# Sixteen tiny copies of zeros behind GpSimd's end-stage stores in a forward and backward decoder step

## The chip, the cores and the metric

The kernel runs on one core of a Trainium2 chip. The core has five instruction streams that run side by side and meet only at semaphores: TensorE (PE), VectorE (DVE), ScalarE (ACT), GpSimd (POOL) and SyncE (SP). Transfers between the chip's memory and the on-chip buffers, and from memory to memory, are carried by sixteen transfer engines. GpSimd and SyncE issue nearly all transfers here. The metric is the device time of one execution in microseconds, and less is better.

## The reference

The reference is one decoder step with adaptive layer norm and the gradient of it. Cut to what matters:

```python
mod = silu(c) @ w_mod                      # six vectors of 1024
sa, ca, ga, sb, cb, gb = split(mod, 6)
h = layernorm(x) * (1 + ca) + sa
q = h @ wq                                 # 32 heads of 128, one query
k, v = k_cache[:, :, -4096:], v_cache[:, :, -4096:]   # of 65536 rows, 4 groups
x = x + ga * (softmax(q k^T / sqrt(128)) v @ wo)
h = layernorm(x) * (1 + cb) + sb
x = x + gb * ((sigmoid(h @ w_gate) * (h @ w_up)) @ w_down)
return x, vjp(x)(grad_out)                 # gradients of ten inputs
```

The gradients of the two caches are as large as the caches, 4 x 65536 x 128 bfloat16 each. Only the last 4096 rows of each group have gradients that are not zero; all other rows must be written with zeros. The weight gradients are outer products of a column and a row.

## The kernel before, in words

**What is written.** Some 186 MB are written and 88 MB read. Most of what is written are the zeros of the two cache gradients, `out_2` (for k) and `out_3` (for v); then come the outer products `out_4` (`wq`), `out_5` (`wo`), `out_6` and `out_7` (`w_gate`, `w_up`), `out_8` (`w_down`) and `out_10` (`w_mod`). The step is for a single token, so all matrix products have one vector on one side.

**Zeros.** `zero` (L184 to 211) writes the zero rows a MiB at a time. The first ten pieces come from an on-chip buffer of zeros; from then on they are copied from memory to memory, out of `zero_src`, a piece of `out_2` that has been filled by then. Six pieces are *narrow*: the cursor that says on which transfer engine the next transfer of few rows starts is reset (L191), a copy of five rows (L193) and one of 60 rows (L197) follow. The pieces are spread over the whole kernel by tables of counts, each tied to a matrix product or a vector instruction that has to be done first. All are written before the end stage.

**The end stage.** From about 512 us on, what is left are weight gradients and the gradients of the live cache rows. Each is made in an on-chip buffer and stored whole, 1 MiB or half of one. These names matter below (line numbers of the profile):

- `sec(j)` (L1249, store at L1253): VectorE makes four of the six sections of row block j of the `w_mod` gradient; GpSimd stores 1 MiB.
- `dwq_tile(j)` (L1299, store at L1301): row block j of the `wq` gradient, 1 MiB.
- `s2(j)` (L1303, store at L1305): the other two sections of the `w_mod` gradient, 512 KiB.
- `grad_kv` (L1282): 32 small matrix products, each copied out of its bank by ScalarE (for v) or by ScalarE and VectorE in turn (for k) at L1292 or L251. A function `between` is called ahead of each one, and it puts other stores between them.
- `kv_store` (L1296, store at L1297): 1 MiB of the finished cache gradient of one group.

For v, `dv_between` runs `sec(4)` and `dwq_tile(0)` ahead of product 8, `sec(5)` and `dwq_tile(1)` ahead of 16, `sec(6)` and `dwq_tile(2)` ahead of 24; four `kv_store` follow, then `sec(7)` and `dwq_tile(3)`. For k, `dk_between` runs:

```python
        if t_ == 4:
            dwq_tile(4)
            s2(0)
            s2(1)
        elif t_ == 10:
            dwq_tile(5)
            s2(2, tail)
            s2(3, tail)
        elif t_ in (18, 25):
            g = (t_ - 4) // 7
            dwq_tile(4 + g, tail)
            s2(2 * g, tail)
            s2(2 * g + 1, tail)
```

`tail` is SyncE's queue; without it a store is GpSimd's. At the end, two `kv_store` of `out_2` are GpSimd's and two SyncE's.

**What sets the order.** Every engine runs its instructions in the order in which they are written down. Buffers are places in one large on-chip area, used again by hand: VectorE waits ahead of an outer product until the store that last read the place has landed. `sec(7)` and then `s2(3)` and `s2(4)` share such a place. The completion semaphores of GpSimd's DMAs form a ring of eight: each DMA takes the next one and first waits until the DMA that had it before has landed, so at most eight of GpSimd's DMAs are under way. SyncE has a ring of eight of its own.

Of the kernel before, what the change touches and what calls it, by code (L numbers as in the profile page):

```python
# [61 lines left out]
def kernel(  # L62
# [26 lines left out]
    nc = tc.nc  # L89
# [19 lines left out]
    def vt(shape, name, dt=FP32):  # L109
        n = shape[1] if dt == FP32 else (shape[1] + 1) // 2  # L110
        if dt not in (FP32, BF16) or n > 48:
            return pool.tile(shape, dt, name=name)
        a = slab[1]
        slab[1] += n
        assert slab[1] <= slab[0].shape[1], slab
        v = slab[0][:, a:a + n]
        return v if dt == FP32 else v.bitcast(BF16)[:, 0:shape[1]]
# [4 lines left out]
    ZW = 4096  # L122
# [15 lines left out]
    def fill_rows(og, g):  # L138
        return og[0, g, 0:SKW, :].rearrange("r d -> (r d)")

    first_rows = fill_rows(out_2, 0).rearrange("(p x) -> p x", p=P)
# [9 lines left out]
    zero_src = flat.pop(0)  # L151
# [6 lines left out]
    narrow = zregions[0:len(NARROW)]  # L158
    zleft = []
# [9 lines left out]
    assert nlen * 2 <= 20  # L169

    keep = [0]
    from_dram = [False]
    zero_rows = zero_src[:, 0:P * ZW // 4].rearrange("i (p x) -> (i p) x", p=P).bitcast(FP8)

# [9 lines left out]
    def zero(n, after=None, big=False):  # L184
        for _ in range(n):
            if len(zleft) <= keep[0]:
                return
            region, narrow_ = zleft.pop(0)
            first = None
            if narrow_:  # L190
                nc.gpsimd.inc_swdge_sem([], [], mode="reset_dge_cursor")  # L191
                n = nlen - ncount.pop()
                first = nc.gpsimd.dma_start(  # L193
                    out=rest[0:NS, 0:nlen * 128].rearrange("p (t x) -> p t x", t=2)[:, :, n * 64:(n + 1) * 64],
                    in_=(zero_rows[0:NS, 0:128].rearrange("p (t x) -> p t x", t=2) if from_dram[0] else
                         zeros[0:NS, 0:64].rearrange("p (t x) -> p t x", t=1).broadcast_to([NS, 2, 64])))
                ins = nc.gpsimd.dma_start(  # L197
                    out=pairs(region[8:P, :].bitcast(FP32)),
                    in_=(pairs(zero_rows[0:120, :]) if from_dram[0] else
                         zeros[0:60, :].rearrange("p (t x) -> p t x", t=1).broadcast_to([60, 2, ZW // 2])))  # L200
            elif big and region.shape[0] == 1:
                ins = nc.gpsimd.dma_start(  # L202
                    out=as_rows(region, BIGP).bitcast(FP32),
                    in_=zero_src[:, 0:P * ZW // 4].rearrange("i (p x) -> (i p) x", p=BIGP).bitcast(FP8))
            else:
                if region.shape[0] == 1:
                    region = as_rows(region, P)
                if from_dram[0]:
                    ins = nc.gpsimd.dma_start(out=pairs(region.bitcast(FP32)), in_=pairs(zero_rows))  # L209
                else:  # L210
                    ins = nc.gpsimd.dma_start(out=region.bitcast(FP32), in_=zeros[:, :])
            if after is not None:
                dep(first or ins, after)
# [26 lines left out]
    def mulv(out, a, b):  # L240
        return tt(out, a, b, ALU.mult)
# [12 lines left out]
    def ttr(out, w, b, acc):  # L254
        return nc.vector.tensor_tensor_reduce(out=out, in0=w, in1=b, scale=1.0, scalar=0.0,  # L255
                                              op0=ALU.mult, op1=ALU.add, accum_out=acc)
# [13 lines left out]
    def matvec_T(blk, cols, name):  # L270
        ncol = cols.shape[2]
        ps = new_acc("mv_" + name)
        for jb in range(KD):
            for nb in range(KD):
                nc.tensor.matmul(ps[:, jb * ncol:(jb + 1) * ncol], lhsT=blk(jb, nb),
                                 rhs=cols[:, nb, :], start=(nb == 0), stop=(nb == KD - 1))
        half = ncol // 2
        v = ps[:, 0:KD * ncol].rearrange("p (j n) -> p j n", j=KD)
        res = vt([P, KD * half], name)
        r = res.rearrange("p (j n) -> p j n", j=KD)  # L280
        cp(r, v[:, :, half:ncol])
        addv(r, r, v[:, :, 0:half])
        return r
# [4 lines left out]
    def outer_dve(out, col, b):  # L288
        return ts(out, b, col, ALU.mult)
# [219 lines left out]
    jobs = []  # L509
# [212 lines left out]
    for g in range(G):  # L722
# [29 lines left out]
        for k in range(2):  # L752
            nc.tensor.matmul(nbank[k][:, :], lhsT=nkb_rows[:, :], rhs=bd[:, 4 * k:4 * k + 4, :].rearrange("p h d -> p (h d)"),
                             start=False, stop=True)
            c0 = (HG * g + 4 * k) * P
# [9 lines left out]
    bq = []  # L765
# [483 lines left out]
    def sec(j):  # L1249
        w5 = g_t[j]  # L1250
        ttr(w5, w5, dmod_b4[:, 3 * D:4 * D], dcs[:, j:j + 1])
        outer_dve(sec_t[j], cs_col[:, j:j + 1], dmod_b4)
        nc.gpsimd.dma_start(out=dwm_view[:, j, 2 * D:6 * D], in_=sec_t[j])  # L1253
# [25 lines left out]
    def kv_out(og, g):  # L1279
        return og[0, g, SKW:, :].rearrange("(p t) d -> p (t d)", t=KT)  # L1280

    def grad_kv(rows, bd, scale, home, engs, between=lambda t_: None):  # L1282
        for t_ in range(KT):
            between(t_)
            tc_, t8 = divmod(t_, 8)
            r = slice(32 * tc_, 32 * tc_ + 32)
            ps = new_ps("ps_kv")
            nc.tensor.matmul(ps[:, :], lhsT=rows[r, t8 * P:(t8 + 1) * P], rhs=bd[r, :], start=True, stop=True,  # L1288
                             tile_position=(32 * tc_, 0))
            o, v = home[:, :, t_ * P:(t_ + 1) * P], ps.rearrange("p (g d) -> p g d", g=G)  # L1290
            if engs[t_ % len(engs)] == "A":
                nc.scalar.activation(out=o, in_=v, func=ACT.Copy, scale=float(scale))  # L1292
            else:
                ts(o, v, float(scale), ALU.mult)

    def kv_store(og, home, g, queue=nc.gpsimd):  # L1296
        queue.dma_start(out=kv_out(og, g), in_=home[:, g, :])  # L1297

    def dwq_tile(j, queue=nc.gpsimd):  # L1299
        outer_dve(dwq_t[j], h1[:, j:j + 1], dq_b)  # L1300
        queue.dma_start(out=dwq_view[:, j, :], in_=dwq_t[j])  # L1301
# [7 lines left out]
    for b in range(2):  # L1309
        do4 = new_ps("do4")  # L1310
        for i in range(KD):
            for a in range(4):
# [4 lines left out]
                       in_=do4.rearrange("q (a h r) -> q a h r", a=4, h=4))  # L1317
# [94 lines left out]
    def dv_between(t_):  # L1412
        if t_ == 8:
            sec(4)
            dwq_tile(0)
        elif t_ == 16:
            sec(5)
            dwq_tile(1)
        elif t_ == 24:
            sec(6)  # L1420
            dwq_tile(2)

    grad_kv(P_b2, DO_bd, 1.0, dv_home, "A", dv_between)
    for g in range(3):
        kv_store(out_3, dv_home, g)
    dln1 = vt([P, KD], "dln1")
    mulv(dln1, dh1, ca1)
    dx0b, _ = layernorm_bwd_col(dln1, ln1, rstd1, "ln1b")
# [2 lines left out]
    bcast(dmod_bf[:, 0:16], 16, dmod_b2, "A")  # L1431
    dcs01 = matvec_T(lambda jb, nb: w01_T[:, nb, jb * P:(jb + 1) * P], dh1_hl, "dcs01")
    kv_store(out_3, dv_home, 3)
    sec(7)
    dwq_tile(3)
    x2 = vt([P, KD], "x2")
    mulv(x2, gb, ffn)
    addv(x2, x2, x1)
# [36 lines left out]
        kv_store(out_2, dk_home, g, nc.gpsimd if g < 2 else tail)  # L1475
    keep[0] = 0
    zero(len(zleft))
    assert not zleft and not narrow and not jobs and not bq

# [1 line left out]
_INS = ['A_x', 'A_k_cache', 'A_v_cache', 'A_wq', 'A_wo', 'B_x', 'B_w_gate', 'B_w_up', 'B_w_down', 'c', 'w_mod', 'grad_out']  # L1481
# [26 lines left out]
```

## Time and profile before

The time is 592.95 us, the median of two runs (592.76 and 593.14).

| What | Value |
|---|---|
| Profiled execution: its time | 593.15 us |
| Profiled execution: its span | 591.4 us |
| PE, DVE, ACT, POOL busy | 426.5, 353.6, 247.9, 147.3 us |
| Bytes moved by DMA, mean rate | 246.05 MB, 416 GB/s |
| Read from and written to memory | 88.52 MB, 185.60 MB |
| GpSimd's queue (q0): packets, MB, share of 16 engines | 26864, 225.98, 94.8% |
| SyncE's and ScalarE's queues (q1, q10) | 4944 and 48 packets, 19.41 and 0.01 MB, 9.3% and 0.0% |

The span reaches from the first instruction to the last; the time also holds what lies around it. A queue's share is the time that its packets took, out of sixteen engines over the whole span; both queues use the same sixteen engines. The time of a store "to landing" runs from its issue to its completion, and so holds the time that it stands in line behind older stores. In the prediction below, a timeline line has start, duration, engine, line in the kernel, operation, tiles, count, and in brackets how long the engine stood idle before it and what ended that. A line of the stretches has the stretch, its length, busy time and instructions of PE, of its weight loads, of DVE, ACT and POOL, then the granted TensorE clock, the share of the DMA engines and GB/s.

### The profile page before, as it was taken

The numbers are of one execution on the slowest core, as the hardware profiler recorded it, in microseconds if no ns is written. First come the engines' busy times: TensorE is split into PE (matmuls) and PEld (weight loads), VectorE is DVE, ScalarE is ACT, GpSimd is POOL, SyncE is SP. The second block draws the span as 40 slices with busy tenths as digits, with TensorE's granted clock in tenths as the row PEclk, the third lists the DMA queues.
The fourth block names the chain that finished last, engine by engine and source line by source line (L and its number), as shares of the span: only waits on it lengthen the run. The fifth ranks groups of instructions, "written<-read, shape, count | busy, mean of one in ns | idle before, by whom it ended". The sixth has DMA issues, their size and how long they took to land.

```text
span 591.4 us, 10184 instructions
## 1 busy us (share of the span) xinstructions
PE 426.5 (72%) x4167; PEld 245.7 (42%) x4196; DVE 353.6 (60%) x644; ACT 247.9 (42%) x398; POOL 147.3 (25%) x250
## 2 busy tenths in 40 slices
PE   3997779999999999997976856767664447075410
PEld 2784433332334545543544645555552435013100
DVE  3665679988830102039371866877986968555750
ACT  2579511554540103411223655666581456084310
POOL 3112214122122212222222321333212533222100
PEclk9998689999999999998997667786876558555555
DMA  8999999999999999999999999999999999999997
GB/s 348 421 418 423 418 457 423 426 432 434 422 401 462 408 444 427 405 433 442 421 377 414 417 412 410 399 409 402 422 418 423 426 426 423 424 419 415 414 416 313
DMA packets 31903, 246.05 MB, mean 416 GB/s; under 512 B 4765, under 2 KB 4765, under 8 KB 16544
## 3 DMA queue, kind: packets, MB, share of 16 engines
q0 software_dynamic: 26864, 225.98, 94.8%
q1 hardware_dynamic: 4944, 19.41, 9.3%
q8 instruction: 33, 0.54, 0.4%
q14 instruction: 14, 0.11, 0.0%
q10 hardware_dynamic: 48, 0.01, 0.0%
HBM read 88.52 MB, written 185.60 MB: 464 GB/s over the span
## 4 chain that ended last, share of the span: by engine, by line
DMA 36%; PE 27%; DVE 18%; ACT 9%; issue 5%; POOL 1%; ACTq 0%; POOLq 0%; DVEq 0%
DMA out_dram<-out_dram 13%; DMA out_dram<-arena 10%; PE n_ps L733 9%; DMA arena<-in_w_mod_dram 6%; DMA arena<-in_B_w_gate_dram 6%; DVE arena L255 5%; PE b_ps L792 4%; DVE arena L251 4%; PE t_ps L687 4%; DVE scr L255 3%; ACT arena L1292 3%; ACT arena L526 2%; DVE arena L238 2%; ACT arena L695 1%; PE tp_k L505 1%
## 5 line engine op out<-in xcount | busy, mean ns | idle before, releaser
L792 PE MATMUL b_ps<-arena 128*128 128x512 bf16 x493 | 115.3, 382 | 2.6 <-ACT arena L936 1.1
L238 DVE TENSOR_TENSOR arena<-arena 128x2048 bf16<-128x2048 bf16 (+1 forms) x67 | 78.2, 1177 | 9.0 <-PE n_ps L733 5.2
L936 ACT COPY arena<-tp_side 128x1024 bf16<-128x1024 bf16 x62 | 60.8, 1017 | 49.7 <-PE tp_side L935 49.0
L792 PEld LDWEIGHTS <-arena 128*128 128x128 bf16 x512 | 48.7, 99 | 57.6 <-issue 4.6
L733 PE MATMUL n_ps<-arena 128*128 128x512 bf16 x247 | 66.5, 389 | 3.4 <-DVE arena L238 2.5
L202 POOL DMA_DIRECT2D out_dram<-out_dram x72 | 35.7, 496 | 129.5 <-PE n_ps L733 49.6
L251 DVE TENSOR_SCALAR arena<-arena,slab 128x3584 bf16<-128x3584 bf16 (+2 forms) x40 | 43.4, 1120 | 24.1 <-DMA out_dram<-arena 24.1
L935 PE MATMUL tp_side<-ident_bf,arena 128*128 128x128 bf16 x496 | 49.7, 265 | 8.9 <-DVE arena L238 4.5
L935 PEld LDWEIGHTS <-arena 128*128 128x128 bf16 x496 | 41.3, 122 | 17.7 <-issue 9.2
L1288 PE MATMUL ps_kv<-arena 32*128 32x512 bf16 x64 | 26.6, 581 | 28.5 <-DVE arena L259 11.7
L695 ACT CAST arena<-t_ps 128x512 bf16<-128x512 f32 x56 | 28.9, 598 | 39.9 <-PE t_ps L687 39.9
L1292 ACT ACTIVATE arena<-ps_kv 128x512 bf16<-128x512 f32 x48 | 25.0, 723 | 38.8 <-PE ps_kv L1288 19.7
L255 DVE CUSTOM_DVE_ANT_0 arena<-arena,scr 128x1024 bf16<-128x1024 bf16 x35 | 40.8, 1219 | 0.2
L733 PEld LDWEIGHTS <-arena 128*128 128x128 bf16 x256 | 21.5, 99 | 35.4 <-issue 18.9
L255 DVE CUSTOM_DVE_ANT_0 scr<-arena,b1k 128x1024 bf16<-128x1024 bf16 x28 | 34.2, 1222 | 3.1 <-DMA arena<-in_B_w_down_dram 2.6
L247 DVE CAST arena<-b_ps 128x512 bf16<-128x512 f32 x6 | 4.1, 692 | 48.9 <-PE b_ps L792 48.9
L209 POOL DMA_DIRECT2D out_dram<-out_dram x32 | 19.5, 610 | 33.6 <-DVE rows_all L238 25.2
L687 PE MATMUL t_ps<-arena 128*32 128x512 bf16 x256 | 24.1, 399 | 3.3 <-ACT arena L756 2.8
L1288 PEld LDWEIGHTS <-arena 32*128 32x128 bf16 x64 | 6.8, 112 | 47.1 <-issue 46.4
L526 ACT COPY arena<-tp_wq 128x1024 bf16<-128x1024 bf16 x23 | 21.4, 1070 | 7.3 <-PE tp_wq L524 7.3
L1073 ACT COPY arena<-tp_ug 128x1024 bf16<-128x1024 bf16 x21 | 20.5, 1007 | 7.5 <-PE tp_ug L1072 7.5
L1049 PE MATMUL fg<-arena,slab 128*32 128x256 bf16 x224 | 15.1, 404 | 8.2 <-DMA arena<-in_B_w_gate_dram 8.2
(266 smaller groups left out, 649.3 us busy)
## 6 DMA issues: line engine op xcount, KB each, us to landing
out_dram<-arena POOLq DMA_DIRECT2D x35, 1024.0 KB, 14.6
out_dram<-out_dram POOLq DMA_DIRECT2D x32, 1024.0 KB, 12.8
out_dram<-arena POOLq DMA_DIRECT2D x16, 896.0 KB, 17.5
out_dram<-zeros POOLq DMA_DIRECT2D x10, 1024.0 KB, 10.3
arena<-in_A_wq_dram POOLq DMA_DIRECT2D x8, 1024.0 KB, 20.9
arena<-in_A_wo_dram POOLq DMA_DIRECT2D x8, 1024.0 KB, 13.7
arena<-in_w_mod_dram POOLq DMA_DIRECT2D x7, 1024.0 KB, 18.9
arena<-in_B_w_up_dram POOLq DMA_DIRECT2D x14, 512.0 KB, 10.1
```

The source lines that it names most:

```text
L202: ins = nc.gpsimd.dma_start(out=as_rows(region, BIGP).bitcast(FP32), in_=zero_src[:, 0:P * ZW // 4].rearrange("i (p x) -> (i p) x", p=BIGP ...
L238: return nc.vector.tensor_tensor(out=out, in0=a, in1=b, op=op)
L251: return nc.vector.tensor_scalar(out=out, in0=a, scalar1=s1, scalar2=None, op0=op0)
L255: return nc.vector.tensor_tensor_reduce(out=out, in0=w, in1=b, scale=1.0, scalar=0.0, op0=ALU.mult, op1=ALU.add, accum_out=acc)
L687: nc.tensor.matmul(ps[32 * hh:32 * hh + 32, :].rearrange("p (j m) -> p j m", j=4), lhsT=N_sb[:, h * P + a:(h + 1) * P - 3 + a:4], rhs=a4[: ...
L695: nc.scalar.copy(out=o, in_=v)
L733: mm = nc.tensor.matmul(nbank[k][:, :], lhsT=k_nat[:, g, t_ * DH:(t_ + 1) * DH], rhs=vp[:, t_ % 2, 4 * k:4 * k + 4, :].rearrange("p h d -> ...
L792: mm = nc.tensor.matmul(bbank[p][k][:, :], lhsT=a4[:, p, h, :], rhs=wo_t[u][:, a, k * 512:(k + 1) * 512], start=(i == 0 and a == 0), stop= ...
L935: nc.tensor.transpose(tp[:, i * P:(i + 1) * P], blk[:, i * P:(i + 1) * P], ident_bf[:, :])
L936: nc.scalar.copy(out=blk if dst is None else dst, in_=tp[:, :])
L1288: nc.tensor.matmul(ps[:, :], lhsT=rows[r, t8 * P:(t8 + 1) * P], rhs=bd[r, :], start=True, stop=True, tile_position=(32 * tc_, 0))
L1292: nc.scalar.activation(out=o, in_=v, func=ACT.Copy, scale=float(scale))
```

## The change

A helper `mark` is added. It issues one copy from memory to memory, on GpSimd's queue: out of `zero_src` into rows 0 to 16 of the first group's zero area in `out_2`, which hold zeros already. Each of the 17 rows has two runs of n elements of two bytes. n is 3 for the first copy and grows by one to 18 for the sixteenth, and each copy has a place of its own. With the first call the engine cursor is reset. A copy with 17 rows is meant to go whole to one transfer engine, and the next copy to the next engine.

The calls stand behind `sec(4)` to `sec(7)`, behind `dwq_tile(0)` to `dwq_tile(3)` and behind the four `kv_store` of `out_3`: twelve in all. Four more follow the last of these, so that there are five in a row ahead of `dwq_tile(4)`. No instruction is taken out. On the other engines the order of instructions is the same; on GpSimd there are seventeen instructions more. Sixteen copies are twice the ring of eight, so the DMAs behind the last copy have the semaphores that they had before. The waits of VectorE and SyncE are for the same stores as before.

```diff
     keep = [0]
+    marks = []
+
+    def mark():
+        if not marks:
+            nc.gpsimd.inc_swdge_sem([], [], mode="reset_dge_cursor")
+        n = 3 + len(marks)
+        c0 = 7 * ZW + 1024 * len(marks)
+        marks.append(n)
+        nc.gpsimd.dma_start(out=first_rows[0:17, c0:c0 + 1024].rearrange("p (k x) -> p k x", k=2)[:, :, 0:n],
+                            in_=zero_src[:, 0:17 * 256].rearrange("i (p k x) -> (i p) k x", k=2, x=128)[:, :, 0:n])
...
     def dv_between(t_):
         if t_ == 8:
             sec(4)
+            mark()
             dwq_tile(0)
+            mark()
         elif t_ == 16:
             sec(5)
+            mark()
             dwq_tile(1)
+            mark()
         elif t_ == 24:
             sec(6)
+            mark()
             dwq_tile(2)
+            mark()
 
     grad_kv(P_b2, DO_bd, 1.0, dv_home, "A", dv_between)
     for g in range(3):
         kv_store(out_3, dv_home, g)
+        mark()
...
     kv_store(out_3, dv_home, 3)
+    mark()
     sec(7)
+    mark()
     dwq_tile(3)
+    mark()
+    mark()
+    mark()
+    mark()
+    mark()
```

## The prediction

> **What bounds the kernel now.** I read the DMA rows of the page first, because the work is mostly stores. Of 16 transfer engines 94.8% of the span goes to the packets of GpSimd's queue and 9.3% to those of SyncE's.
>
> ```profile
> DMA  8999999999999999999999999999999999999997
> q0 software_dynamic: 26864, 225.98, 94.8%
> q1 hardware_dynamic: 4944, 19.41, 9.3%
> q10 hardware_dynamic: 48, 0.01, 0.0%
> ```
>
> The row of tenths stays at nine from the second slice to the last but one, so the sum of bytes over the rate of the engines sets the time, and an instruction that is late costs something only where the engines run dry. Next I cut the end stage into stretches (column after POOL: granted TensorE clock, DMA share, GB/s).
>
> ```profile
> 520.00:530.00 10.00, 9.28 (x19) 1.88 (x19) 5.90 (x6) 9.92 (x21) 2.34 (x3) 0.50 1.02 421
> 555.00:560.00 5.00, 0.37 (x1) 0.10 (x1) 2.37 (x4) 0.00 (x0) 0.00 (x0) 0.50 1.00 413
> 583.00:585.00 2.00, 0.00 (x0) 0.00 (x0) 0.00 (x0) 0.00 (x0) 0.00 (x0) 0.50 1.00 408
> 585.00:587.00 2.00, 0.00 (x0) 0.00 (x0) 0.00 (x0) 0.00 (x0) 0.00 (x0) 0.50 0.87 367
> 587.00:588.00 1.00, 0.00 (x0) 0.00 (x0) 0.00 (x0) 0.00 (x0) 0.00 (x0) 0.50 0.53 221
> 589.00:590.00 1.00, 0.00 (x0) 0.00 (x0) 0.00 (x0) 0.00 (x0) 0.00 (x0) 0.50 0.12 49
> ```
>
> The engines are full to 585 us and then fall out one by one; 0.12 of 16 is two engines that carry the last microsecond. Third comes GpSimd's timeline, with what it waited for.
>
> ```profile
> 525.68 1.02 POOL L1253 DMA_DIRECT2D out_dram<-arena  x1 [7.14 <-DVE arena L251]
> 529.22 1.02 POOL L1253 DMA_DIRECT2D out_dram<-arena  x1 [1.81 <-DVE arena L251]
> 530.41 0.53 POOL L1301 DMA_DIRECT2D out_dram<-arena  x1 [0.18 <-DVE arena L238]
> 536.15 2.10 POOL L1297 DMA_DIRECT2D out_dram<-arena  x4 [5.21 <-ACT arena L1292]
> 540.03 1.02 POOL L1253 DMA_DIRECT2D out_dram<-arena  x1 [1.77 <-DVE arena L251]
> 548.60 0.53 POOL L1301 DMA_DIRECT2D out_dram<-arena  x1 [6.84 <-DVE arena L251]
> ```
>
> Asking for each of these stores alone gives its time from issue to landing: 16.1 us for the first `dwq_tile` (518.0), 11.0 for `sec(5)` (525.7), 12.3 for `dwq_tile(1)` (526.9), 17.6 for `sec(7)` (540.0), 19.7 for `dwq_tile(3)` (541.2). Added to the issues, the landings come every 2.5 to 2.8 us from 528.9 to 557.6, as 1 MiB at 416 GB/s (2.5 us) must. What they wait for is each other. The chain says last where a landing holds an engine:
>
> ```profile
> 540.03 17.57 DMA out_dram<-arena
> 557.60 0.03 issue
> 557.63 6.28 DVE arena L251 x9
> ```
>
> `s2(3)` on VectorE overwrites the buffer of `sec(7)` and may start when that store has landed; the last four stores follow from there at 570.1 to 571.1, and land by 590.5. At 570 the engines still have about 8 us of older work, so that chain could slip by some microseconds for nothing. The bound is the transfer engines.
>
> **The change, part by part.** Nothing is removed. Added on GpSimd: one cursor reset, and sixteen copies of 17 rows by two runs of 3 to 18 bfloat16, thus 34 packets of 6 to 36 bytes each.
>
> *GpSimd's time.* The reset is one instruction; the six like it take 18 ns each. A narrow copy of 10 runs takes 601 ns (row of L193), a plain one of three rows 522 (L417); I take 0.6 us, so sixteen are 9.6 us. Between 516.8 and 571 GpSimd is busy some 15 us, so it has the room. If it had not, each copy would delay the store behind it by 0.6 us.
>
> *Waits.* In the program every GpSimd DMA takes one of eight completion semaphores in turn and first waits for that semaphore's last user. The copies take places in this ring, so from `dwq_tile(0)` on a big store waits for the big store four before it, not eight. With the old landings the new issues are: `sec(6)` when `sec(4)` lands, 531.4 (529.2 before); `dwq_tile(2)` 534.1 (530.4); the four stores of `kv_store` 536.7, 539.2, 542.0, 544.7 (536.2 to 537.7); `sec(7)` 547.3 (540.0); `dwq_tile(3)` 549.8 (541.2); after the last five copies `dwq_tile(4)` at 557.6 (548.6), with `s2(0)`, `s2(1)` and `dwq_tile(5)` behind it in GpSimd's queue up to 561. Nobody but the end waits for these four. Until `sec(7)`, three or four big stores are in flight at each of these issues. Before, at 525.7, there were four as well, and the stretch 520 to 530 above shows a share of 1.02 and 421 GB/s: four are enough. So `sec(7)` lands where it did, and VectorE's chain holds, each later only by what the copies take from the engines.
>
> *The one thin place.* When `dwq_tile(4)` is let go, only `dwq_tile(3)` (2.5 us of work) and SyncE's first half-megabyte store (553.3 to 562.3) are under way. An issue takes 0.5 to 1.0 us on GpSimd and then has to reach the engines, which I bound by as much again; so 1.0 to 2.0 us against a cover of 2.5 and more. I take 0.2 us; without the cover it is 2.0. SyncE's waits are unchanged.
>
> *The engines' time.* If the copies go to the sixteen engines in turn, each engine gets 34 small packets once, and a completion for each of sixteen copies (the page counts 4765 packets under 512 B for about 280 DMAs, some 16 or 17 each). What a tiny store packet costs no row shows. From below: the mean packet of q1 is 19.41 MB / 4944 = 3926 B and takes 9.3% x 16 x 591.4 us / 4944 = 178 ns, of which the bytes need 150 at the 26.1 GB/s of one engine (422 GB/s at a share of 1.01), so 28 are left; in q0 it is 334 ns for 8412 B, 12 left. Bytes aside, 34 x 12 ns = 0.4 us, or nothing if they fit between others. From above: q10's 48 packets, 256 B and less, round to 0.0%, at most 0.05% x 16 x 591.4 = 4.7 us, 99 ns each, so 3.4 us; they are the nearest row. A packet cannot well cost more than q1's 178 ns, 6.1 us, unless each waits for memory. I take the middle of 28 and 99, 63 ns: 34 x 63 = 2.1 us, and 16 completions x 28 ns = 0.4 us. Every engine gets the same, so the two that end last end 2.5 us later.
>
> [...]
>
> *Sum.* 2.5 + 0.2 = 2.7 us on the profiled execution's 593.15 us (span 591.4 and 1.75 around it): 595.85. Its time is 0.2 above the median of the runs, 592.95, so for the median I say 595.65, rounded 595.7.
>
> **Rivals.**
>
> *The copies vanish (not slower).* For it: the share runs to 1.02, so packets of the two queues overlap, and 34 x 21 B is no traffic. Against it: full engines have no idle time to give before 585 us. Price: 0 to 0.4 us, so 592.9 to 593.3. It decides if a tiny packet costs under 12 ns.
>
> *Each tiny write waits.* [...] For it: `out_dram<-out_dram` has memory at both ends, as the copies have, unlike q10. Against it: those 1 MiB copies run at full share, so their reads overlap. At q1's 178 ns it is 6.1 + 0.4 + 0.2 = 6.7 us: 599.7; at double that price, about 606.
> [...]
>
> *Too few in flight (slower).* If the engines need the seven stores of the steady stretch (latency 17.5 us there) and not four, the twelve stores after 518 flow at 4 MiB in 17.5 us, 4.4 us each and not 2.5: 12 x 1.9 = 23 us, so 616. For it: GpSimd's issues really come up to 9 us later. Against it: the 1.02 at 525 us with four in flight. It decides once landings stand more than 2.7 us apart while four are out.
>
> *The copies don't go round (slower).* If the cursor stays, all sixteen meet on one engine: 544 x 63 ns = 34 us there, partly hidden if it is an early one, so about 620 to 627. No row tells for or against it: the kernel's six pairs of a five-row and a 60-row copy go through the same cursor, and the share of 1.0 to 585 us shows only that they left no engine far behind. If a copy were spread over all engines, each would still get 34 packets and the forecast stands.
> [...]
>
> **How the numbers follow.** Forecast 0.57, with a range of its own from 594.0 to 597.5; vanishing 0.17; waiting writes 0.19; too few in flight 0.04; one engine 0.03. The range 592.6 to 600.6 takes in the forecast's whole range, most of the vanishing case and the lower half of the waiting one, some 0.8 together. A measurement of this kernel can tell about 2%, 11.9 us, from no change. Over that lie the last two rivals, nearly whole, and the far end of the waiting one: slower 0.06. Faster by so much needs bytes taken away, and none are: 0.01. Within 2%: 0.93.
>
> **What the profile of the changed kernel would show.** Right: GpSimd's issues of `sec(7)` and `dwq_tile(4)` near 548 to 550 and 558 to 561, each after a wait for a landing; landings of big stores falling to 10 to 11 us after issue; a DMA share of 1.0 through 585 us; q0 about 800 packets more, the last engines done near 592.5. Wrong: a share under 0.97 between 555 and 565 (the thin place is real), landings over 2.7 us apart with four stores out, the end at 591.5 or less (the copies vanish), at 596 or more (they wait).

## The result, and the profile after

The changed kernel takes 601.61 us (median of two runs, 601.31 and 601.90) against 592.95: a ratio of 1.0144, 95% interval 1.0127 to 1.0161, or 8.7 us more where 2.7 were forecast. It lies just above the stated range. The profiled span is 599.5 us, 8.1 more. All times here and below are of undisturbed executions; two of the four of the kernel with double the runs took 992 and 1984 us, and they are left out.

The page, with the same rows as before, and the row of packet counts:

```profile
DMA  9999999999999999999999999999999999999997
DMA packets 32415, 246.10 MB, mean 410 GB/s; under 512 B 5266, under 2 KB 5277, under 8 KB 17056
q0 software_dynamic: 27376, 226.03, 94.6%
q1 hardware_dynamic: 4944, 19.41, 9.4%
```

The engines look as busy as before. But 94.6% of the longer span is 9074 us of packet time in q0, where it was 94.8% of 591.4, 8970: some 104 engine-microseconds more, for 0.05 MB. The stretches say where (the last two columns are DMA share and GB/s). First a line of the kernel before, then the changed kernel:

```profile
530.00:555.00 25.00, 14.68 (x112) 6.97 (x111) 15.28 (x40) 13.52 (x26) 6.55 (x12) 0.50 1.01 414
```

```profile
530.00:555.00 25.00, 14.52 (x111) 6.87 (x110) 16.04 (x40) 13.36 (x26) 13.40 (x17) 0.50 1.00 359
562.00:564.00 2.00, 0.00 (x0) 0.00 (x0) 0.02 (x1) 0.00 (x0) 0.00 (x0) 0.50 0.92 223
564.00:566.00 2.00, 0.02 (x1) 0.01 (x1) 2.00 (x4) 0.00 (x0) 1.15 (x2) 0.50 0.58 134
595.00:596.00 1.00, 0.00 (x0) 0.00 (x0) 0.00 (x0) 0.00 (x0) 0.00 (x0) 0.50 0.28 115
597.00:598.00 1.00, 0.00 (x0) 0.00 (x0) 0.00 (x0) 0.00 (x0) 0.00 (x0) 0.50 0.08 33
```

Before, the stretch from 530 to 555 had a share of 1.01 and 414 GB/s. Now the share is still 1.00 and the rate 359: the engines count as full and move fewer bytes. From 562 to 566 they are not full; the missing shares are 0.08 x 2 + 0.42 x 2 = 1.0 us on the mean engine. GpSimd's timeline shows the same stores as before, and one of the copies (L180):

```profile
532.47 0.55 POOL L1263 DMA_DIRECT2D out_dram<-arena  x1 [1.92 <-DMA out_dram<-arena]
533.05 0.98 POOL L180 DMA_DIRECT2D out_dram<-out_dram  x1
535.64 0.55 POOL L1311 DMA_DIRECT2D out_dram<-arena  x1 [1.61 <-DMA out_dram<-arena]
538.76 0.94 POOL L1307 DMA_DIRECT2D out_dram<-arena  x1 [1.57 <-DMA out_dram<-arena]
551.32 0.55 POOL L1263 DMA_DIRECT2D out_dram<-arena  x1 [1.83 <-DVE arena L261]
564.54 0.59 POOL L1311 DMA_DIRECT2D out_dram<-arena  x1 [2.66 <-DMA out_dram<-out_dram]
```

These are `sec(6)`, the copy behind it, `dwq_tile(2)`, the first `kv_store`, `sec(7)` and `dwq_tile(4)`. For `sec(7)` the profile names VectorE, but VectorE had made that block by 540.8; the store eight places ahead in the ring, the first `kv_store`, landed at 550.8. One by one, the big stores land at 531.9 (`sec(4)`), 535.1, 538.3, 541.3, 544.2, 547.5, 550.8, 553.3, 556.3, 559.7, 563.9 (`sec(7)`): about 0.5 us later with every store and its copy, beginning with the first. The chain keeps its shape:

```profile
551.32 12.64 DMA out_dram<-arena
563.96 0.02 issue
563.98 6.27 DVE arena L261 x9
```

`s2(3)` starts at 563.98, where it was 557.63.

### The profile page after: what moved, and what is told of

It is laid out like the page before. It is cut to its first block, busy times and chain, and to the rows that moved or that the text cites. A ratio compares the mean times of both kernels' runs of the same rounds, so it can differ in the third digit from the quotient of the medians.

```text
span 599.5 us, 10201 instructions
## 1 busy us (share of the span) xinstructions
PE 426.5 (71%) x4167; PEld 244.6 (41%) x4196; DVE 354.4 (59%) x644; ACT 248.0 (41%) x398; POOL 164.4 (27%) x266
## 2 busy tenths in 40 slices
DMA packets 32415, 246.10 MB, mean 410 GB/s; under 512 B 5266, under 2 KB 5277, under 8 KB 17056
## 3 DMA queue, kind: packets, MB, share of 16 engines
q0 software_dynamic: 27376, 226.03, 94.6%
## 4 chain that ended last, share of the span: by engine, by line
PE 36%; DMA 30%; DVE 18%; ACT 6%; issue 5%; POOL 1%; ACTq 0%; POOLq 0%; another core or an unknown queue 0%; DVEq 0%; SPq 0%
DMA out_dram<-arena 12%; PE b_ps L802 11%; PE n_ps L743 9%; DMA out_dram<-out_dram 7%; DVE arena L261 5%; DMA arena<-in_B_w_gate_dram 5%; PE t_ps L697 3%; DVE arena L265 3%; DMA arena<-in_w_mod_dram 3%; DVE scr L265 3%; PE ps_kv L1298 3%; DMA arena<-in_B_w_down_dram 2%; ACT arena L536 2%; DVE arena L248 2%; ACT arena L705 1%
## 5 line engine op out<-in xcount | busy, mean ns | idle before, releaser
L971 POOL DMA_DIRECT2D arena<-in_B_w_up_dram x14 | 10.9, 781 | 38.6 <-DVE slab L265 24.1
```

## The experiments

Three theories stood after this. A, later called P: each tiny run holds its one engine some 190 ns (104 engine-microseconds over 544 runs). B: four stores in flight are too few. C: each copy costs all engines half a microsecond; later narrowed to Q, a price for a copy that is whole on one engine. The last one, M (mirror: a copy on one engine puts as many descriptors on the other fifteen), came from the first eight results. A descriptor here means an engine's work for one run; a packet, as the profile counts it, can hold many: the 34 runs of 6 B of the change's first copy are one packet of 204 B. All edits are to the changed kernel's `mark`; where a time is "over before", it is the difference to the runs of the kernel before on the same chip.

**One run in place of 34.** The ring is used as in the change, with next to nothing to move.

```diff
-  out=first_rows[0:17, c0:c0 + 1024]...[:, :, 0:n], in_=...
+  out=first_rows[0:1, c0:c0 + 256], in_=zero_src[:, 0:256]
```

> The sixteen copies stay in their places in GpSimd's queue and in its ring of eight semaphores, but each moves one run of 512 B in place of 34 short ones. Theory A (each short run holds its transfer engine about 190 ns, 34 of them 6.5 us, and the thin place ahead of dwq_tile(4) costs the rest): at most 1 to 2 us over before, 593.5 to 595. Theory B (only four big stores are in flight, and the engines need more): all of the loss stays, 600 to 602. Theory C (each copy costs all engines half a microsecond, whatever is in it): 600 to 602 too.

593.73 us against 593.03, 1.0020 (1.0008 to 1.0032): 0.7 us. B falls, and a price for every copy whatever it holds falls too. The stretches of this kernel:

```profile
530.00:555.00 25.00, 14.41 (x111) 6.88 (x110) 15.02 (x38) 13.25 (x26) 11.29 (x18) 0.50 1.01 411
550.00:560.00 10.00, 3.79 (x10) 1.27 (x11) 5.68 (x9) 2.36 (x5) 4.39 (x8) 0.50 0.93 373
```

With four big stores in flight the rate is 411 GB/s; only the last stretch has a hole, 0.07 x 10 = 0.7 us. That is the thin place. In the trace, the one run of 512 B is sixteen packets of 32 B for each copy (256 in all), so no copy of this kernel has its data in one packet, and Q is not tested by it.

**Runs of 512 B.**

```diff
-  ...[:, :, 0:n], in_=zero_src[:, 0:17 * 256]...x=128)[:, :, 0:n]
+  ...[:, :, 0:256], in_=zero_src[:, 0:17 * 512]...x=256)
```

> The same 34 runs to a copy, each lengthened to 512 B. Theory A with the cost from runs that are too short (a write that must first be read): each run costs about its bytes, 20 to 30 ns, so 34 of them 1 us: 594 to 596. Theory A with a fixed price per run, short or not: 601 to 603. Theories B and C: 600 to 603.

601.92 us, 1.0149 (1.0134 to 1.0164), as the change: the length of the runs that carry data makes no difference here, with 8.9 us over before at 512 B and 8.7 at 6 to 36. That is a weaker test than it looks, as the packet sizes below show.

**Read from on-chip zeros.**

```diff
-  in_=zero_src[:, 0:17 * 256]...
+  in_=do_pad[0:17, 8:8 + n]...broadcast_to([17, 2, n])
```

> The same short runs with the same destinations, but read from on-chip zeros and not from memory. Theory A with the price on the write side: unchanged, 601 to 602. Theory A with the price on the read side (each run waits for a read of memory): 594 to 596. B and C: 600 to 602.

601.60 us, 1.0146 (1.0130 to 1.0163). The read of the data from memory is not the price.

**16 rows in place of 17.**

```diff
-  out=first_rows[0:17, ...], in_=zero_src[:, 0:17 * 256]...
+  out=first_rows[0:16, ...], in_=zero_src[:, 0:16 * 256]...
```

> 16 rows in place of 17, so that each copy is split over all sixteen engines, two runs on each. Over sixteen copies an engine gets 32 runs in place of 34. Theory A with a price per run: 600.5 to 601.5, since the total for an engine is the same. Theory A with a price per copy on its one engine (a long stall in one place): less, 595 to 598, if two runs stall less than 34. B and C: 600 to 602.

593.85 us, 1.0014 (1.0003 to 1.0024): 0.8 us, hardly more than the ring alone. The packets agree that each copy is split: all 512 new ones are under 512 B (5277 - 4765 of the page), where the change has 11 larger ones. With nearly the same number of runs over the kernel, the price is gone. Either 34 runs in a row on one engine are another thing than two (P), or a copy that is whole on one engine costs more than its runs (Q).

**All engines 34 runs, once.**

```diff
+  if len(marks) == 12:
+      ...out=first_rows[0:16, 7 * ZW:7 * ZW + 34 * 256]...k=34)[:, :, 0:10]
```

> One copy in place of sixteen, ahead of the last store of kv_store for v's neighbour sec(7)... that is, in the place of the twelfth copy: 16 rows of 34 runs, so that every engine gets its 34 short runs at once and one behind the other; one place of the ring of eight. Theory P (a run costs about 190 ns where many stand one behind the other on an engine): 6.5 us once for all engines, 599 to 600. Theory Q (the price belongs to a copy that lies whole on one engine, about half a microsecond for everything each time): no such copy is left, 593 to 594.

593.23 us against 592.97, 0.9998 (0.9988 to 1.0008). Of its 32 new packets sixteen have 512 B to 2 KB (4797 - 4781 of the page), and 34 runs of 20 B for each of sixteen engines are sixteen times 680 B. 34 short runs one behind the other on every engine cost under 0.5 us. P falls.

**17 runs, and 68.**

```diff
+  half:   ...k=2)[:, 0:1, 0:n]
+  double: ...k=4)[:, :, 0:n]
```

> The sixteen copies in their places, each with one run to a row, 17 in place of 34. P: half of 6.5 us and the 1.2 us that the places in the ring cost: 597 to 598. Q: unchanged, 601 to 602. If only a stall beyond what the engine is ahead counts, less than P, 594 to 596.

> The sixteen copies in their places, each with four runs to a row, 68 in place of 34. P: 13 us and 1.2 us: 606 to 608. Q: unchanged, 601 to 602.

Half: 594.01 us, 1.0024 (1.0013 to 1.0036). Double: 608.5 and 609.4 us, 1.0265 (1.0245 to 1.0286). Double costs 15.9 us, as a price for each run would have it, so Q falls as it was put; but half costs only what the ring costs, which fits no price per run. The packet counts gave the next theory. First the row of the kernel before, then that of the double one:

```profile
DMA packets 31903, 246.05 MB, mean 416 GB/s; under 512 B 4765, under 2 KB 4765, under 8 KB 16544
```

```profile
DMA packets 32671, 246.14 MB, mean 406 GB/s; under 512 B 5518, under 2 KB 5530, under 8 KB 17312
```

The change adds 512 packets, 16 x 32, as many as two for each engine and copy. Only 11 of them have 512 B or more (5277 - 5266), and 11 of the copies hold that much (34 runs of 16 B and up): so the data of a copy are one packet. Double adds 768, 16 x 48, three for each engine and copy, and runs of 512 B add 1536, 16 x 96, six. The packets beside the data grow in number with the runs. That is M, if they lie on the other fifteen engines.

The trace keeps the size of each packet, though not its engine. For each copy the change has one packet with the data of all 34 runs (204 B for the first copy, 1224 for the last) and fifteen packets of 136 B (240 in all), 34 times 4 B; the other 256 new packets, 16 a copy, have 4 B each and are taken here for completions (the kernel before has 4065 of 4 B in q0). The double kernel has 240 of 256 B and 240 of 16 B, 64 and 4 times 4 B. With runs of 512 B the data lie in packets of 4096 B (eight runs) and 1024 B (two), and there are 960 packets of 32 B and 240 of 8 B, eight and two times 4 B. What fits all three is fifteen times 4 B beside every run; such 4 B are called a *filler* here. That they lie on the fifteen engines without data is a reading of the number fifteen, and of the times below; no trace names a packet's engine.

This also shows what the kernels with longer runs and with an on-chip source could tell: they changed the packets of data and nothing else. Their fillers, fifteen times 4 B for each of 34 runs, add up to those of the change, so a price of short runs could still stand in the fillers.

Of the 100 engine-microseconds that the packets of q0 add up to over before, the copies' own packets hold 50, and 49 of them are in the 240 packets of 136 B (204 ns on average; 14 of the 16 data packets took 44 to 48). Most of the rest is in the 8 KiB packets of q0 that start after 530 us: 339 ns on average, where it was 317.

**Written to an on-chip buffer** (into columns of `do_pad` that hold zeros).

```diff
+  out=do_pad[p0:p0 + 17, x0:x0 + 8]..., in_=zero_src...[:, :, 0:4]
```

> The copies read the same 34 short runs from memory (8 bytes each) but write them into an on-chip buffer that holds zeros, not into out_2. If the price lies in the write to memory: 594 to 595. If it lies in the count of descriptors on one engine, whatever they move: 601 to 602.

601.50 us, 1.0140 (1.0125 to 1.0155): the write of the data to memory is not the price either. Here too there are 240 packets of 136 B.

**Sixteen copies, each with 34 runs for every engine.**

```diff
+  out=first_rows[0:16, c0:c0 + 2040]...k=34)[:, :, 0:n]
```

> Sixteen copies in the places of the change, with 16 rows of 34 runs each: now every transfer engine really carries 34 short runs in every copy, sixteen times the runs of the change. Theory M (mirror: a copy that lies whole on one engine puts as many descriptors on the other fifteen, so the change already gave every engine 34 in every copy, 544 in all, at 14 ns): the same as the change, 601 to 602. Theory P (190 ns a run, on one engine only): 16 x 6.5 us, near 690. Theory Q (a price for a copy that is whole on one engine): there is none here, 594.

600.78 us against 593.14, 1.0129 (1.0114 to 1.0144). Sixteen times the work at no more time than the change. The packet row:

```profile
DMA packets 32415, 246.24 MB, mean 411 GB/s; under 512 B 5101, under 2 KB 5277, under 8 KB 17056
```

The number of packets is the same to the last one, 32415. Now 176 of them (5277 - 5101) have 512 B or more, 16 x 11: each copy has sixteen packets of data. The change has as many packets, with fillers in fifteen where the wide kernel has data in all sixteen. The wide kernel has no fillers, so it is real runs of 6 to 36 B on every engine that cost as much here; 512 B on every engine was not run. GpSimd takes 0.67 us for a wide copy and 0.98 for one of the change, so its own time is not the price.

**544 runs on every engine, at once.**

```diff
+  if len(marks) == 12:
+      ...out=first_rows[0:16, 7 * ZW:7 * ZW + 544 * 60]...k=544)[:, :, 0:10]
```

> One copy in the place of the twelfth, 16 rows of 544 runs of 20 bytes, so each engine gets all its 544 short runs at once, and one place of the ring is used. Theory M: 544 x 14 ns = 7.6 us on every engine, 600 to 601.5, without the 0.7 us of the ring. Theory P: 544 x 190 ns, near 690. Theory Q: 593 to 594.

608.85 us, 1.0267 (1.0249 to 1.0284): P and Q are out by far, and M's size is missed by a factor of two, 29 ns a run in place of 14. The engines do little else for some 15 us:

```profile
560.00:565.00 5.00, 2.20 (x6) 0.73 (x6) 5.00 (x8) 1.72 (x3) 0.00 (x0) 0.50 1.27 64
565.00:570.00 5.00, 2.71 (x6) 0.67 (x5) 5.00 (x9) 1.79 (x3) 0.00 (x0) 0.50 0.92 52
```

**34 rows of one run.**

```diff
+  out=first_rows[0:34, c0:c0 + n], in_=zero_src[:, 0:34 * 128]...[:, 0:n]
```

> Sixteen copies in their places with 34 rows of one run each. M, if rows alone are dealt out to the engines (as the 17 rows of one run in the half-runs kernel may have been): two or three runs on each engine in each copy, 593.5 to 594.5. M, if such a copy lies on two engines with 17 runs and is mirrored on the others: 16 x 17 x 14 ns = 3.8 us more, 597 to 598. P: with rows dealt out 594, on two engines 597 to 598.

594.21 us, 1.0023 (1.0010 to 1.0035): the ring's price alone. The same 34 runs, as rows, cost nothing measurable, as did 17 rows of one run. The packet sizes show that these rows, of one run each, were dealt out. For the first copy, with runs of 6 B, two packets have 18 B (three runs) and fourteen 16 B (two runs and a filler). With 17 rows of one run it is one packet of 12 B (two runs) and fifteen of 10 B (one run and a filler).

**Twelve copies.**

```diff
+  if len(marks) <= 12:
```

> The four last copies are left out, so transfer engines 12 to 15 carry none, and dwq_tile(4) waits for the second store of kv_store and not for sec(7). M: all engines pay for twelve copies, 12 x 34 x 14 ns = 5.7 us, and the thin place is gone: 598.5 to 599. P with the price on the marked engine alone: 593.5 to 594 if the engines that end last are among 12 to 15, else the whole 6.5 us, 599.5 to 601.

599.12 us, 1.0102 (1.0087 to 1.0117): 6.0 us, of which M asked 5.7 (it is 0.1 above M's range). Which engines the four copies left out would have taken, no run shows. `dwq_tile(4)` is issued at 557.4, and the hole is gone:

```profile
530.00:555.00 25.00, 14.99 (x112) 6.97 (x111) 16.45 (x40) 13.84 (x27) 13.96 (x17) 0.50 1.00 356
555.00:560.00 5.00, 0.00 (x0) 0.00 (x0) 0.00 (x0) 0.00 (x0) 1.90 (x3) 0.50 1.00 346
560.00:565.00 5.00, 0.00 (x0) 0.00 (x0) 0.90 (x2) 0.00 (x0) 1.06 (x2) 0.50 1.00 369
```

**17 runs on every engine; eight rows of 34; four copies of 136.**

```diff
+  first_rows[0:16, ...]...k=34)[:, 0:17, 0:n]
+  first_rows[0:8, ...]...k=34)[:, :, 0:n]
+  if len(marks) in (3, 6, 9, 12): ...k=136)[:, :, 0:10]
```

> Sixteen copies in their places, 16 rows of 17 runs, so each engine really carries 17 short runs in every copy. Theory M with one price for every run: 16 x 17 x 14 ns = 3.8 us and 0.7 to 1 us for the places in the ring, 597.5 to 598. If only runs beyond some number that other packets hide cost anything: 593.5 to 595.

> Sixteen copies in their places, 8 rows of 34 runs, so that eight engines carry runs in each copy and eight carry none. M: the other eight get as many descriptors all the same, so like the change, 600.5 to 602. Without a mirror, each engine carries 34 runs in every second copy: half, 597 to 598.

> The same 544 runs of 20 bytes for each engine, in four copies of 16 rows by 136 runs behind the third, sixth, ninth and twelfth big store, in place of all at once. If the 29 ns a run of the single copy come from their standing alone on the engines, with no big store beside them: between 14 and 29 ns, 601 to 607. If they come from the narrower spacing of the runs (120 B), which is the same here: 608 to 609. Price of 14 ns: 601.

17 runs: 595.92 us against 592.98, 1.0052 (1.0034 to 1.0070). 48 of its new packets have 512 B or more (5277 - 5229 of the page), 16 x 3, as 17 runs on each of sixteen engines do for the three longest sizes. Less 0.9 us for the ring (the kernels that only use its places pay 0.7 to 1.1) it is 2.0 us, 7.5 ns a run: between the two forecasts, as if the first runs of a copy were cheaper. Eight rows: 599.40 us, 1.0103 (1.0085 to 1.0120), between M's range and that without a mirror, in neither. The time alone leaves it open; its packets decide:

```profile
DMA packets 32416, 246.16 MB, mean 412 GB/s; under 512 B 5190, under 2 KB 5278, under 8 KB 17057
```

Once more some 512 packets more, but 88 with 512 B and over, 8 x 11: each copy has eight packets of data, and beside them eight of fillers (128 packets of 136 B in all). So the packets that M asks for are there, but the price is 10 ns a run, (6.4 - 0.9) / 544; why it is less than with data in one packet or in sixteen stays open. Four copies: 601.06 us, 1.0139 (1.0120 to 1.0158), 14.9 ns a run with the narrow spacing and the same number of runs. So the spacing is not what made 544 at once dear; that leaves their standing together.

## Why the prediction was wrong

**The engines' time: wrong, and the reason for the miss.** The step that failed is "each engine gets 34 small packets once". Packets and times fit 16 x 34 = 544 on each engine: the data of a copy are one packet (204 to 1224 B), the fifteen beside it have 136 B each, 34 fillers, and the wide copies, with 34 real runs in each of sixteen packets, cost 7.6 us over before where the change costs 8.7. The price was mis-sized the other way: 63 ns a run was taken, 14 was measured: (8.7 - 0.9) / 544, where 0.9 is the middle of the 0.7 to 1.1 us that the places in the ring cost alone; in the same way 13.8 from the double copies and 12.4 from the wide ones, and 6.0 / 408 = 14.7 from the twelve, which have no hole. So 34 x 63 ns = 2.1 us stood for 544 x 14 = 7.6 us. The count of packets was off too, 512 more and not 800, since many runs go into one (34 in 204 B). Of the two bounds from packet rows, the one from below, 12 ns out of q0, lies near the 14, which is luck: it was worked out for a packet, and 14 is for a run. q10's 99 ns was a bound and not a neighbour.

**The sentence that hid it.** "If a copy were spread over all engines, each would still get 34 packets and the forecast stands" counts runs. What fits the times here is the longest share of any engine in each copy, times the number of copies. The wide copies show it: sixteen times the runs in 0.8 us less.

**Waiting writes: wrong mechanism near the right time.** The rival at 599.7 us came within 2 us. But it asked 178 ns of each run, and 34 runs at once on every engine cost under 0.5 us, less than 15 ns each; 544 at once cost 29 each. Runs of 512 B, a source on the chip and a destination on the chip change nothing (601.92, 601.60 and 601.50 us), but they change the data alone. What a filler of 4 B does in its 14 ns, no run shows.

**Too few in flight: rightly set low.** One run in place of 34 leaves four stores in flight and 411 GB/s. Landings 3 us apart with four stores out, which the prediction gave as its mark, do stand in the changed kernel's trace; the mark was a poor one, for engines that are full and move less give the same picture.

**Waits and order: right.** The stores wait where it was said; `sec(7)` at 551.3 and `dwq_tile(4)` at 564.5 are 4.0 and 6.9 us later than worked out, about the lateness that the copies had gathered by then (the landings they wait for are 3.5 and 6.3 us late). GpSimd's time was short: 0.98 us for a copy of 34 runs and not 0.6, without effect.

**The thin place: right, but too small.** 0.2 us were taken, up to 2.0 allowed; the hole is 1.0 us in the changed kernel, and the kernels that have the ring's places alone pay 0.7 to 1.1. Where `dwq_tile(4)` may go one landing earlier it is gone.

**The copies go round: one packet for each is right, the turn is not shown.** One packet of data a copy is what the trace shows for 17 rows of two runs, and the count of 11 agrees; 17 rows of one run were dealt out over sixteen packets. Which engine has the data, and whether the cursor's reset or the next copy changes it, no run shows.

## What to carry to other kernels

When small GpSimd copies are added to a stretch bound by the transfer engines, count for each copy the runs on its fullest engine and charge them to all sixteen. Here that gave the time of the change, the double and the twelve copies at 14 to 15 ns a run; a copy with its data in one packet was not a sixteenth of the load. Deal the same bytes out evenly instead: 16 rows in place of 17 took 0.8 us where 17 took 8.7. A busy share of 1.00 with a rate of 359 GB/s in place of 414 meant many small descriptors here, and the rows of packet counts, by size, told over how many packets the data were dealt out.

## What the runs showed of the hardware that was not expected

- The data of a GpSimd copy of 17 rows by two runs were one packet (204 to 1224 B in the changed kernel); beside it stood fifteen packets of 136 B, 4 B for every run, and sixteen of 4 B. With 34, 68 and 34 x 512 B the copies added 2, 3 and 6 packets for each engine and copy (512, 768 and 1536 in all). Where each copy has eight packets of data there are eight of 136 B beside them (128 in all). On which engine each lies, no trace says.
- GpSimd copies of 17 and 34 rows with one run each were dealt out: sixteen packets for the data of the first copy, of 10 and 12 B and of 16 and 18 B, the smaller ones with a run less and one filler. They pay none of this: 594.0 and 594.2 us.
- A tiny run or filler, counted on the fullest engine of each copy, cost 14 ns of the kernel's time between big stores in the change: 12 with runs of 6 to 36 B in sixteen packets a copy, 10 with eight packets of data, 7.5 where only 17 come together, and 29 where 544 do. In the change, half of the added packet time stands in the small packets themselves (50 of 100 engine-microseconds); the 8 KiB packets beside them take longer, 339 ns where it was 317. Why the price grows with the number in a row stays open.
